# Two feed-forward layers behind a retention layer: when the weights' preparations are opened, and what stands ahead of what in the queues

## The chip, the cores and the metric

The kernel runs on one core of one Trainium2 chip. The metric is the device time of one execution in microseconds (us). One execution of the kernel was also profiled. TensorE (PE) does the matrix products, VectorE (DVE), ScalarE (ACT) and GpSimd (POOL) the elementwise work, and SyncE (SP) issues most DMA transfers. ACT issues some too, between its own instructions. Each engine works through its own instructions strictly in order, so an instruction that waits holds up everything behind it on that engine.

## The reference

A retention layer (attention with a decaying state, 4 sequences of 768 positions, 8 heads of 64) is followed by two feed-forward layers (3072 tokens, model width 512, hidden width 2048), all in float32:

```python
state = gamma[None, :, None, None] * state + np.einsum('bhd,bhe->bhde', k[:, :, t], v[:, :, t])
y[:, :, t] = scale * np.einsum('bhd,bhde->bhe', q[:, :, t], state)
...
x = attn_out.transpose(0, 2, 1, 3).reshape(B * S, H * D)
h = x @ w_in;  x = np.maximum(0.01 * h, h) @ w_out              # first layer
h = x @ w_in2; y = (h / (1.0 + np.exp(-1.702 * h))) @ w_out2    # second layer
```

## The kernel before

**Retention** runs in 24 steps of 128 positions. A step loads its q, k and v (1 MB, `a_load`) into one of the areas w4 to w7, which later hold weights. `a_scores` makes the masked scores of a step one step ahead, `a_decay` scales the keys on ACT, `a_out` makes the outputs and the new state, and `a_store` scales the outputs on DVE and, for all but the first sequence, writes them to DRAM with three transfers (`swapped`). `place(s)` says in which area a step's data stand: four areas in turn for the first eight steps, three (w5, w6, w7) after that. So a load is issued four steps ahead at first and three steps ahead later. The first seven steps run alone; the other 17 are fed in half steps between the products of the first layer.

**Each layer** has two stages. In `First`, the inputs times `w_in` go through the activation function and are stored to DRAM. In `Second`, those times `w_out`. Both use a scheme that multiplies 2 x 2 blocks with seven products of sums of blocks in place of eight; every float32 operand is split in a high and a low part, and a product takes three matmuls for each half of the inner dimension, six in all. `First` has 32 pairs (4 blocks of tokens, times 8 blocks q of the hidden width) of seven products each. I call one product, with the evacuations of PSUM behind it, a tick, because the function `tick` is called once behind each. In the first five pairs of the first layer (`one`) the products of a pair use each other's banks closely and the retention's half steps stand between them. From pair 5 on, the products of a pair and of the one before are interleaved, 1, 5, old 7, 2, 6, old 3, old 4. A copy on ACT (L479) of the first product's bank must be made before product 2 may add to that bank, and an add on DVE (L403) combines two banks. Before products of a new block begin, `early_sums` makes two sums of its inputs on POOL (L335, L336), at the pair q = 6.

**A weight's preparation** (`Prep`, one for each half of each block q, 16 for each of the four weight matrices) turns a stored 64-bit word into float32 and forms the seven sums of blocks. Its steps are: `load` (two transfers of 256 KB into a raw buffer), `open` (two ACT instructions, L169 and L170, that read the raw buffer and write into a result buffer), `word` (three DVE instructions, L173, L175, L177), `round_up` (one POOL instruction, L186, the last to read the raw buffer), `total` (three subtractions, L152 when on DVE or POOL) and then `store` (448 KB to DRAM), or `keep` (a cast on ACT, L155, and a subtraction on DVE, L152, straight into the weight's area), or `split` and `store_split` (a high and a low part in two result buffers, and two stores). Raw and result buffers are taken in turn from rings: in the first layer two, later three raw buffers and three result buffers (areas c1, ex and c2), in the second two raw and three result buffers.

The order of all this is written out by hand. `Later` is a table of steps that are due at a tick. The weights of the first layer's `First` (`own`, 16 preparations) have ticks of their own (`OWN_AT`: load, words with sums, keep). Of the other 48, 26 are made during the first layer's `First` and 22 during the second's. They come in bunches: `TODO1` and `TODO2` say at which pair one or two preparations are put into a queue (`behind`) as three pieces each, `open`, two of the `word` steps, and the third with rounding, sums and the `load` of a later preparation. One piece is taken from the queue at each tick, except in the pairs at a block's end and beginning. The store or keep follows five ticks behind the third piece.

```python
            def finish():
                self.word(2, 3)
                self.sums(e, e2)
                self.end(clock, keep)
                if others:
                    others.pop(0).load()

            return [self.open, lambda: self.word(2), finish]
```

`sums` is `round_up` on POOL and `total` right behind it: on DVE for the first layer's 26 and the second's first few, on POOL for `own` and for the rest.

Of the kernel before, what the change touches and what calls it, by code (L numbers as in the profile page):

```python
# [21 lines left out]
P = 128  # L22
# [16 lines left out]
def _word(bits):  # L39
# [20 lines left out]
EARLY_PREPS = ((3, 5), (4, 6))  # L60
EARLY_FORMS = ((1, 3), (2, 4), (5, 5), (6, 6))
OWN_AT = {2: (None, 0, 2), 3: (None, 2, 4), 4: (3, 6, 8), 5: (5, 8, 10), 6: (8, 11, 13), 7: (12, 15, 17), 8: (16, 19, 21),
          9: (20, 23, 25), 10: (23, 26, 31), 11: (26, 29, 32), 12: (28, 31, 34), 13: (30, 34, 38), 14: (32, 37, 42),
          15: (35, 41, 44)}
# [35 lines left out]
def retention_two_ffn(ctx: ExitStack, tc: tile.TileContext, qkv, consts, small, w1i, w1o, w2i, w2o, scratch, out):  # L100
# [87 lines left out]
    class Prep:  # L188
# [37 lines left out]
        def sums(self, e=nc.gpsimd, e2=None):  # L226
            round_up(self.f, self.low, e)
            self.total(e2 or e)

        def words(self):  # L230
            self.open()
            self.word(3)

# [16 lines left out]
        def end(self, clock, keep=False, ticks=5):  # L250
# [8 lines left out]
        def pieces(self, clock, others, e, e2, keep=False):  # L259
            def finish():  # L260
                self.word(2, 3)
                self.sums(e, e2)
                self.end(clock, keep)
                if others:
                    others.pop(0).load()

            return [self.open, lambda: self.word(2), finish]
# [432 lines left out]
    def early(s):  # L700

        for n, (words, keep) in enumerate(EARLY_PREPS):
            if s == words:
                own[n].words()
                own[n].sums()
            if s == keep:
                own[n].keep()
# [9 lines left out]
    def retention():  # L717
        place = lambda s: (5, 6, 7, 4)[s % 4] if s < 8 else 5 + (s - 8) % 3
# [71 lines left out]
        def a_store(s, o):  # L790
# [17 lines left out]
            swapped(xd0[b][:, :, c * P : c * P + P], x)  # L808
# [29 lines left out]
        for s in range(len(steps)):  # L838
# [9 lines left out]
            a_store(s, o)  # L848
# [144 lines left out]
    def step2(n):  # L993
# [4 lines left out]
        if n == 1:  # L998
            for p in todo[:2]:
                p.load()  # L1000
# [137 lines left out]
```

## Time and profile before

| | us |
|---|---|
| two timed executions | 1169.71, 1169.93 (median 1169.82) |
| the profiled execution, its own time | 1171.34 |
| span of its trace | 1169.6 |
| PE busy in it (91%) | 1063.1 |
| DVE busy (67%) | 778.4 |
| ACT busy (53%) | 617.3 |
| POOL busy (17%) | 193.6 |

The span is cut in stages, which follow each other: the first seven retention steps up to about 60 us; the first layer's `First` from 60 to 442, with the other retention steps in it up to about 177; its `Second` to 671; the second layer's `First` from 670.8 to 935.3; its `Second` to the end. A busy PE is no proof of a PE at full pace: matmuls overlap, and at half of the granted clock they take twice as long. So the number of matmuls in a stretch of time is read beside it.

### The profile page before, as it was taken

To read this page: it belongs to the slowest core of one execution; us is meant where nothing else is said; L and a number is where in the kernel's file an instruction comes from. 1 tells how busy PE (TensorE), PEld (TensorE's weight loads), DVE (VectorE), ACT (ScalarE), POOL (GpSimd) and SP (SyncE) were. 2 spreads that over 40 slices of the span, in tenths; PEclk is the share of its full clock that TensorE was granted. 3 is DMA by queue.
4 is the path that set the end of the run, shared out by engine and by line. 5 is a ranking of instruction groups with operands and counts; after the bars stand their busy time and mean duration, and the time that the engine had idled before them with its cause. 6 is when DMAs were issued, how large, how long until landed. Compare 5 with 4: busy or idle time off the path is not lost.

```text
span 1169.6 us, 17536 instructions
## 1 busy us (share of the span) xinstructions
PE 1063.1 (91%) x6150; PEld 943.3 (81%) x6151; DVE 778.4 (67%) x1255; ACT 617.3 (53%) x1223; POOL 193.6 (17%) x193
## 2 busy tenths in 40 slices
PE   8687886968877999999999997989899999999998
PEld 6566665968867998888888897989799988888886
DVE  5855454546546658978878857535343589788786
ACT  5644434635445676555454674645455655454543
POOL 0332126213223100000000003444450000000000
PEclk9988889987988999999999998999999999999999
DMA  8568754387677787372353784486747863753823
GB/s 322 193 208 301 244 178 152 126 279 246 211 252 251 247 304 230 99 248 79 127 187 89 249 284 145 152 287 207 267 177 228 260 198 117 178 154 72 218 73 72
DMA packets 190568, 231.37 MB, mean 198 GB/s; under 512 B 59152, under 2 KB 146192, under 8 KB 187408
## 3 DMA queue, kind: packets, MB, share of 16 engines
q1 hardware_dynamic: 148704, 179.08, 48.5%
q10 hardware_dynamic: 41776, 51.17, 12.2%
q8 instruction: 48, 0.79, 0.3%
q14 instruction: 40, 0.33, 0.1%
HBM read 141.46 MB, written 88.74 MB: 197 GB/s over the span
## 4 chain that ended last, share of the span: by engine, by line
PE 61%; DMA 17%; DVE 9%; ACT 4%; POOL 3%; issue 3%; SPq 1%; ACTq 1%; POOLq 0%; DVEq 0%
PE psum L599 37%; PE psum L374 22%; DMA w<-qkv 6%; DMA wd1o<-c 3%; POOL c L186 2%; DMA e<-w2o 2%; DMA a<-gd 1%; PE psum L747 1%; DVE w L152 1%; DMA c<-w1o 1%; DVE c L177 1%; DMA gd<-b 1%; DVE c L152 1%; DMA wd2i<-c 1%; DMA gd<-f 1%
## 5 line engine op out<-in xcount | busy, mean ns | idle before, releaser
L599 PE MATMUL psum<-c,w 128*128 128x512 f32 x1008 | 229.0, 389 | 0.0
L599 PEld LDWEIGHTS psum<-c,w 128*128 128x128 f32 x1008 | 189.1, 188 | 39.5 <-DVE c L152 0.2
L374 PE MATMUL psum<-a,w 128*128 128x384 f32 x576 | 120.7, 360 | 28.0 <-ACT psum L479 21.8
L374 PEld LDWEIGHTS psum<-a,w 128*128 128x128 f32 x576 | 107.5, 203 | 35.5 <-ACT psum L479 24.8
L599 PE MATMUL psum<-e,w 128*128 128x512 f32 x576 | 135.8, 389 | 0.0
L374 PE MATMUL psum<-c,w 128*128 128x384 f32 x576 | 115.8, 344 | 18.1 <-DVE d L403 17.8
L599 PEld LDWEIGHTS psum<-e,w 128*128 128x128 f32 x576 | 108.1, 188 | 22.4
L374 PEld LDWEIGHTS psum<-c,w 128*128 128x128 f32 x576 | 103.0, 193 | 21.4 <-DVE d L403 20.4
L374 PE MATMUL psum<-b,w 128*128 128x384 f32 x576 | 111.4, 337 | 0.8 <-ACT psum L479 0.8
L374 PEld LDWEIGHTS psum<-b,w 128*128 128x128 f32 x576 | 102.2, 190 | 1.1 <-ACT psum L479 1.1
L374 PE MATMUL psum<-e,w 128*128 128x384 f32 x384 | 81.5, 357 | 15.1 <-DVE b L403 4.8
L374 PE MATMUL psum<-d,w 128*128 128x384 f32 x384 | 83.2, 362 | 10.9 <-ACT w L155 8.5
L552 ACT CAST c<-b 128x512 fp32r<-128x512 f32 x96 | 59.4, 622 | 55.7 <-DVE c L152 30.3
L374 PEld LDWEIGHTS psum<-e,w 128*128 128x128 f32 x384 | 71.0, 201 | 20.0 <-DVE dx L403 6.4
L374 PEld LDWEIGHTS psum<-d,w 128*128 128x128 f32 x384 | 73.0, 205 | 14.8 <-ACT w L155 9.4
L186 POOL TENSOR_TENSOR c<-c,c 128x512 int32<-128x512 int32 x33 | 44.2, 1338 | 226.7 <-DVE c L177 140.4
L152 DVE TENSOR_TENSOR c<-b,c 128x512 fp32r<-128x512 f32 x96 | 65.5, 689 | 18.9 <-ACT c L552 16.9
L393 ACT ACTIVATE d<-psum 128x384 f32<-128x384 f32 x96 | 46.4, 490 | 50.1 <-PE psum L374 44.9
L152 DVE TENSOR_TENSOR w<-w 128x512 fp32r<-128x512 f32 (+3 forms) x102 | 48.1, 511 | 29.9 <-ACT w L288 23.9
L152 DVE TENSOR_TENSOR c<-c 128x128 f32<-128x128 f32 (+1 forms) x82 | 36.8, 449 | 44.8 <-POOL c L186 38.2
L758 ACT ACTIVATE w<-w,f 128x64 f32<-128x64 f32 x160 | 40.4, 335 | 44.2 <-DMA w<-qkv 37.2
L152 POOL TENSOR_TENSOR a<-a 128x768 f32<-128x768 f32 x7 | 13.2, 1890 | 277.3 <-DMA xd<-e 260.4
(200 smaller groups left out, 1779.4 us busy)
## 6 DMA issues: line engine op xcount, KB each, us to landing
gd<-d ACTq DMA_DIRECT2D x128, 192.0 KB, 3.2
w<-qkv SPq DMA_DIRECT2D x21, 1024.0 KB, 6.0
b<-gd SPq DMA_DIRECT2D x72, 256.0 KB, 4.1
d<-gd SPq DMA_DIRECT2D x54, 256.0 KB, 3.7
a<-gd SPq DMA_DIRECT2D x48, 256.0 KB, 4.8
gd<-dx ACTq DMA_DIRECT2D x47, 192.0 KB, 3.5
c<-w1i SPq DMA_DIRECT2D x32, 256.0 KB, 4.6
e<-w2o SPq DMA_DIRECT2D x32, 256.0 KB, 4.0
```

The source lines that it names most:

```text
L152: e.tensor_tensor(out=o, in0=x, in1=y, op=ALU.subtract)
L177: lambda f, high: nc.vector.scalar_tensor_tensor(out=f, in0=f, scalar=3, in1=high, op0=ALU.logical_shift_left, op1=ALU.bitwise_or))
L186: e.tensor_tensor(out=f.bitcast(I32), in0=f.bitcast(I32), in1=low.bitcast(I32), op=ALU.add)
L374: nc.tensor.matmul(out=t, lhsT=w[:, k, a], rhs=x[:, b, k], start=(start and m == 0), stop=(m == 5), skip_group_check=True)
L393: nc.scalar.activation(out=t, in_=x, func=self.func)
L552: nc.scalar.copy(out=t[:, 0], in_=self.block_of(*item))
L599: nc.tensor.matmul(out=t[:, j], lhsT=w[:, j, a], rhs=x[:, b], start=(new and q == 0 and m == 0), stop=(q == NQ - 1 and m == 2), skip_group ...
L747: nc.tensor.matmul(out=ps[:, e, n], lhsT=kT[r, n], rhs=qT[r, n], start=True, stop=True, skip_group_check=True)
L758: nc.scalar.activation(out=ks_t[s][:, h], in_=ks_t[s][:, h], func=AF.Copy, scale=kdec[:, c, h : h + 1])
```

## The change

- `own` preparations: the sums leave POOL for DVE, one or two ticks behind the words and rounding, and the keep follows at the tick of before, or for one of them a tick earlier. In the first steps `own_words` does the same through the table of due steps.
- The other 48 preparations no longer go through the queue. Each has a tick in `OPEN1` (five apart) or `OPEN2` (six, then eight apart), from which `plan` sets every step: the load 7 ticks (first layer) or 5 ticks (second) before, `open`, two word steps one tick later, the third word step and the rounding two ticks later, the sums on DVE four ticks later, the store five (or the keep six, or the split five and its stores seven).
- Retention: `a_load` is written ahead of the store of the same step, and the four areas are used for the first 16 steps.
- The second layer's result ring has two buffers in place of three, and its `First` eight buffers for the activated results (`g`) in place of five.

```diff
-OWN_AT = {2: (None, 0, 2), 3: (None, 2, 4), 4: (3, 6, 8), ...
-          9: (20, 23, 25), 10: (23, 26, 31), 11: (26, 29, 32), 12: (28, 31, 34), 13: (30, 34, 38), 14: (32, 37, 42),
-          15: (35, 41, 44)}
+OWN_AT = {2: (None, 0, 1, 2), 3: (None, 2, 1, 2), 4: (3, 6, 1, 2), ...
+          8: (16, 19, 1, 2), 9: (20, 23, 1, 2), 10: (23, 26, 1, 5), 11: (26, 29, 1, 3), 12: (28, 31, 1, 3),
+          13: (30, 34, 2, 4), 14: (32, 37, 2, 4), 15: (35, 41, 2, 3)}
-TODO1 = {**{n: 2 for n in (9, 10, 11, 12, 13, 14, 17, 18, 19, 20, 21)}, **{n: 1 for n in (22, 25, 26, 27)}}
-TODO2 = {2: 2, 4: 2, 5: 2, 6: 1, 9: 2, 10: 1, 11: 1, 12: 1, 13: 2, 14: 1, 17: 2, 18: 1, 19: 1, 20: 1, 21: 1, 22: 1}
+OPEN1 = (*range(54, 100, 5), *range(109, 157, 5), *range(165, 195, 5))
+OPEN2 = (10, 16, 22, 28, 34, 39, *range(53, 100, 8), *range(109, 158, 8), 165, 173, 181)
...
+        def own_words(self, clock, total, keep):
+            self.open()
+            self.word(3)
+            round_up(self.f, self.low, nc.gpsimd)
+            clock.at(total, lambda: self.total(nc.vector))
+            clock.at(keep, self.keep)
+
+        def last_word(self):
+            self.word(2, 3)
+            round_up(self.f, self.low, nc.gpsimd)
+
+        def plan(self, clock, at, lead, keep=False):
+            clock.at(at - lead, self.load)
+            clock.at(at, self.open)
+            clock.at(at + 1, lambda: self.word(2))
+            clock.at(at + 2, self.last_word)
+            clock.at(at + 4, lambda: self.total(nc.vector))
             if keep:
-                clock.at(ticks, self.keep)
+                clock.at(at + 6, self.keep)
             elif self.kind == "2i" and self.q < N_SPLIT:
-                clock.at(ticks - 1, self.split)
-                clock.at(ticks + 1, self.store_split)
+                clock.at(at + 5, self.split)
+                clock.at(at + 7, self.store_split)
             else:
-                clock.at(ticks, self.store)
+                clock.at(at + 5, self.store)
...
-        place = lambda s: (5, 6, 7, 4)[s % 4] if s < 8 else 5 + (s - 8) % 3
+        place = lambda s: (5, 6, 7, 4)[s % 4] if s < 16 else 5 + (s - 16) % 3
...
-            a_store(s, o)
+            put = a_store(s, o)
             if s + 2 < len(steps):
                 a_decay(s + 2)
-            n = s + 4 if s < 7 else s + 3
-            if s != 7 and n < len(steps):
+            n = s + 4 if s < 15 else s + 3
+            if s != 15 and n < len(steps):
                 a_load(n)
+            if put is not None:
+                put()
...
+    for p, at in zip(todo1, OPEN1):
+        p.plan(later, at, 7)
...
-                    "g": run_of(g_a2, 5, 1.5), "p": run_of(p_a2, 2, 1.5)},
+                    "g": run_of(g_a2, 8, 1.5), "p": run_of(p_a2, 2, 1.5)},
...
-    prep_rings2 = [ring(run_of(pe, 2, 4), 4, P, 2), ring([(pe, 8), (pex, 0), (g_a2, 8)], 8, P)]
+    prep_rings2 = [ring(run_of(pe, 2, 4), 4, P, 2), ring([(pe, 8), (pex, 0)], 8, P)]
...
+    for p, at in zip(todo, OPEN2):
+        p.plan(later2, at, 5, p.kind == "2i")
```

Three places show the order of instructions. Line numbers are a few lower in the changed kernel: L169, L170 (`open`), L173, L175, L177 (`word`), L152 (`total`) and L403 (`add`) of before are L168, L169, L172, L174, L176, L151 and L400 there. `c_315` is the result ring, `c_94` and `ex` are raw buffers, `psum` the banks.

DVE, in the middle of the first layer's `First`, before:

```order
L173 TENSOR_SCALAR c_315<-c_315 128x512
L175 TENSOR_SCALAR ex<-c_315 128x512
L177 SCALAR_TENSOR_TENSOR c_315<-c_315,ex 128x512
L152 TENSOR_TENSOR c_315<-c_315 128x256
L152 TENSOR_TENSOR c_315<-c_315 128x128 x2
```

The same place, changed:

```order
L172 TENSOR_SCALAR c_315<-c_315 128x512
L174 TENSOR_SCALAR ex<-c_315 128x512
L400 TENSOR_TENSOR f<-psum,f 128x384
L176 SCALAR_TENSOR_TENSOR c_315<-c_315,ex 128x512
L400 TENSOR_TENSOR psum<-psum,f 128x384
L151 TENSOR_TENSOR c_315<-c_315 128x256
L151 TENSOR_TENSOR c_315<-c_315 128x128 x2
```

The three subtractions stood right behind the last word step, whose result POOL still has to round. Now an add of the products stands between them.

ACT, in the first layer's last block, where the split preparations are (`L155` before and `L154` changed is the cast of `split`, `w_426` or `w_425` a weight's area), before:

```order
L155 CAST c_315<-c_315 128x896
L386 DMA gd_74<-f 128x384
L288 CAST w_426<-w_426 128x384 x2
L485 COPY f<-psum 128x384
L386 DMA gd_74<-f 128x384
L169 ACTIVATE c_315<-ex 128x512
```

Changed:

```order
L154 CAST c_315<-c_315 128x896
L168 ACTIVATE c_315<-c_94 128x512
L169 ACTIVATE c_94<-c_94 128x512
L476 COPY psum<-psum 128x384
L383 DMA gd_74<-f 128x384
```

The next `open` stands right behind the cast of the split; both write into a result buffer of the same ring.

SP, in the retention beside the first layer (`L737` or `L731` is `a_load`, `L162` and `L164` or `L161` and `L163` the store of a step, `L204` or `L203` a weight's load), before:

```order
L162 DMA xd_1_67<-w_84 256x1x128
L164 DMA xd_1_67<-w_84 128x1x128 x2
L737 DMA w_84<-qkv 128x2048
L162 DMA xd_1_67<-w_79 256x1x128
L164 DMA xd_1_67<-w_79 128x1x128 x2
L737 DMA w_77<-qkv 128x2048
```

Changed:

```order
L731 DMA w_84<-qkv 128x2048
L161 DMA xd_1_67<-w_84 256x1x128
L163 DMA xd_1_67<-w_84 128x1x128 x2
L203 DMA c_94<-w1i 128x2x256 x2
L731 DMA w_77<-qkv 128x2048
L161 DMA xd_0_66<-w_79 256x1x128
```

The load of a later step now stands ahead of the step's own store.

## Rows read from the trace of the kernel before

**Rows 1.** Matmuls of line 374 (products of `First`) alone, in stretches of us.

```profile
184.20:210.40 26.20, 18.70 (x85) 17.27 (x85) 0.87 0.37 119
225.00:292.70 67.70, 53.31 (x253) 50.46 (x252) 0.85 0.79 256
307.30:375.30 68.00, 51.09 (x253) 47.71 (x252) 0.87 0.76 259
397.20:416.20 19.00, 15.65 (x87) 14.46 (x86) 1.00 1.04 385
...
846.50:912.00 65.50, 65.50 (x380) 65.50 (x379) 1.00 0.64 216
670.80:935.30 264.50, 244.05 (x1344) 239.06 (x1343) 0.97 0.66 221
```

**Rows 2.** Waits of ACT, 225 to 375.3: us in total, times, longest.

```profile
ACT c L169 <- DMA wd1o<-c: 30.9, 10, 9.4
ACT c L169 <- DMA wd2i<-c: 11.5, 4, 4.0
ACT c L169 <- DMA c<-w1o: 8.0, 1, 8.0
```

**Rows 3.** Waits of DVE, the same stretch.

```profile
DVE c L152 <- POOL c L186: 33.8, 23, 1.5
```

**Rows 4.** Timeline 245 to 275: start, duration, instruction, [idle before <- releaser].

```profile
249.04 1.07 DVE L152 TENSOR_TENSOR c<-c 128x256 f32<-128x256 f32 x3 [1.46 <-POOL c L186]
...
261.97 0.66 ACT L169 ACTIVATE c<-ex 128x512 f32<-128x512 f32 x1 [4.38 <-DMA wd1o<-c]
...
263.83 0.49 ACT L479 COPY psum<-psum 128x384 f32<-128x384 f32 x1
...
264.38 4.21 PE L374 MATMUL psum<-a,w 128*128 128x384 f32 x12 [2.36 <-ACT psum L479]
```

**Rows 5.** DMA issues: size of each, median us from issue to landing.

```profile
gd<-dx ACTq DMA_DIRECT2D x47, 192.0 KB, 3.5
...
e<-w2o SPq DMA_DIRECT2D x32, 256.0 KB, 4.0
...
wd1o<-c SPq DMA_DIRECT2D x16, 448.0 KB, 5.8
...
c<-w1o SPq DMA_DIRECT2D x22, 256.0 KB, 4.3
```

**Rows 6.** Timeline 719 to 732, POOL and DVE.

```profile
722.82 1.83 POOL L335 TENSOR_TENSOR a<-a 128x768 f32<-128x768 f32 x1
722.90 4.21 DVE L152 TENSOR_TENSOR d<-d 128x256 f32<-128x256 f32 x3 [1.48 <-POOL d L186]
```

**Rows 7.** Waits of ACT, 670 to 935.

```profile
ACT e L169 <- DMA e<-w2o: 11.1, 3, 7.6
ACT ex L169 <- DMA gd<-d: 6.2, 1, 6.2
ACT d L169 <- DMA e<-w2o: 5.4, 2, 3.3
```

**Rows 8.** Timeline 176 to 200, the last keeps of `own`.

```profile
184.61 2.28 POOL L152 TENSOR_TENSOR c<-c 128x256 f32<-128x256 f32 x3
...
187.91 0.62 PE L374 MATMUL psum<-d,w 128*128 128x384 f32 x2 [3.04 <-ACT w L155]
```

**Rows 9.** Waits of PE, 62 to 200.

```profile
PE psum L747 <- DMA w<-qkv: 17.8, 8, 3.9
```

**Rows 10.** Timeline 100 to 132, one retention step's store and the load behind it.

```profile
104.20 0.68 DVE L805 TENSOR_TENSOR w<-psum,f 128x512 f32<-128x512 f32 x1
...
107.39 0.61 SPq L737 DMA_DIRECT2D w<-qkv  x1
```

**Rows 11.** Stretches: busy PE, PEld, DVE, ACT, POOL; granted clock, DMA share, GB/s.

```profile
60.00:176.80 116.80, 95.25 (x1049) 79.68 (x1050) 61.74 (x90) 49.75 (x133) 27.86 (x36) 0.87 0.73 236
...
400.00:420.00 20.00, 16.65 (x92) 15.49 (x92) 12.46 (x24) 13.66 (x28) 1.30 (x1) 1.00 1.03 368
...
30.00:60.00 30.00, 19.00 (x250) 15.36 (x250) 26.19 (x38) 18.79 (x49) 11.93 (x14) 0.93 0.55 178
```

More of the change, by code (lines that the diff above doesn't have):

```diff
@@ L224, in total @@
             subtract(f[:, 7], f[:, b21], f[:, 6], e)
[L226 to L232, printed above, removed]
         def store(self):
@@ L700, in early @@
     def early(s):
-        for n, (words, keep) in enumerate(EARLY_PREPS):
+        for n, words in enumerate(EARLY_PREPS):
             if s == words:
[L704 to L707, printed above, removed]
+                own[n].own_words(later, 1, 2)
         if s in EARLY_LOADS:
@@ L860, in retention_two_ffn @@
             early(k // 2)
-    behind1, todo1, waiting1 = collections.deque(), [], []
+    behind1 = collections.deque()
     for k, i in enumerate(FORMS[4:]):
         first1.form(0, i, (2 * k, 2 * k, 2 * k + 1), e=nc.vector)
-    for n, (load, words, keep) in OWN_AT.items():
+    for n, (load, words, total, keep) in OWN_AT.items():
         if load is not None:
             later.at(load, own[n].load)
-        if words is not None:
-            later.at(words, own[n].words)
-            later.at(words, own[n].sums)
-        if keep is not None:
-            later.at(keep, own[n].keep)
-    todo1.extend(names["1o"] + names["2i"][2 * N_SPLIT : N_IN1] + names["2i"][: 2 * N_SPLIT])
-    def start1(behind, todo, waiting, k, clock, e, e2, keep=lambda p: False):
-        for _ in range(k):
-            if todo:
-                p = todo.pop(0)
-                behind.extend(p.pieces(clock, waiting, e, e2, keep(p)))
+        later.at(words, lambda p=own[n], a=total, b=keep: p.own_words(later, a, b))
+    todo1 = names["1o"] + names["2i"][2 * N_SPLIT : N_IN1] + names["2i"][: 2 * N_SPLIT]
+    assert len(todo1) <= len(OPEN1)
+    for p, at in zip(todo1, OPEN1):
+        p.plan(later, at, 7)
     x_a, y_a, z_a, u_a = [[(Area(t), n) for t, n in k] for k in
@@ L896, in step1 @@
             first1.g = ring(run_of(g_a[0], 2, 1.5) + run_of(few, 2, 1.5, 3) + (run_of(g_a[1], 2, 1.5) if n == 28 else []), T1)
-        if n in (6, 7):
-            for p in todo1[0:2] if n == 6 else todo1[2:3]:
-                p.load()
-            waiting1[:] = todo1[3:]
-        if n in TODO1:
-            start1(behind1, todo1, waiting1, TODO1[n], later, nc.gpsimd, nc.vector)
         if n == 26:
@@ L922, in retention_two_ffn @@
         behind1.popleft()()
-    assert not todo1 and not waiting1
     SPLITS2 = {3: [(6, 6, 7)], 4: [(7, 6, 7)], 10: [(6, 3, 4)], 11: [(7, 3, 4)], 18: [(6, 0, 1)], 19: [(7, 0, 1)],
@@ L988, in retention_two_ffn @@
     later2.at(2, lambda: w_split(2, 2, 3))
[L989 removed]
+    behind = collections.deque()
     todo = [Prep("2i", n, prep_rings2) for n in range(N_IN1, 2 * NQ)] + [Prep("2o", n, prep_rings2) for n in range(2 * NQ)]
[L991 removed]
+    assert len(todo) == len(OPEN2)
+    for p, at in zip(todo, OPEN2):
+        p.plan(later2, at, 5, p.kind == "2i")
     def step2(n):
@@ L997, in step2 @@
             behind.extend(w_steps(n + 2, 3, 7) + w_steps(n + 2, 0, 3))
-        if n == 1:
-            for p in todo[:2]:
-                p.load()
-            waiting.extend(todo[2:])
-        if n in TODO2:
-            start1(behind, todo, waiting, TODO2[n], later2, nc.gpsimd, nc.vector if n < 6 else nc.gpsimd,
-                   lambda p: p.kind == "2i")
         if n == 26:
@@ L1010, in retention_two_ffn @@
         behind.popleft()()
-    assert not todo and not waiting
     ident = t_a.view(0, P)
```

17 lines of the change are left out of this document (3 added, 14 removed).

## The prediction

> **What bounds the kernel now.** PE sets the end: outside of a few places its next matmul waits for nothing but the one before. So I read first how fast the products of `First` go, stretch by stretch, by their count. In the second layer 380 matmuls take 65.5 us, nine pairs, with PE busy throughout and a granted clock of 1.00 [rows 1]: 65.5 / 9 = 7.28 us for a pair, 1.04 for a tick. Held against that, the same work is late elsewhere [rows 1]:
>
> - first layer, pairs 10 to 15 (67.7 us) and 18 to 23 (68.0), six pairs each: 67.7 + 68.0 - 12 x 7.28 = 48.3 us lost;
> - pairs 6 and 7: 26.2 - 14.6 = 11.6 lost;
> - two pairs in the last block: 19.0 - 14.6 = 4.4 lost;
> - the whole `First` of the second layer: 264.5 - 32 x 7.28 = 31.5 lost.
>
> The clock column belongs to this: 0.85 to 0.87 in the bad stretches. A stall is followed by matmuls at half clock, and both are in the sums above.
>
> Next, who is late. In the two bad stretches ACT waits at `open`, 50.4 us in all over three rows [rows 2], nearly what PE loses there. Most is for the store of a preparation (wd1o, wd2i) that still reads the result buffer. The releaser's row with c<-w1o is a load. DVE waits 23 times for the rounding on POOL, 33.8 us [rows 3], with the adds of the products queued behind. One instance shows the whole chain [rows 4]: `open` at 261.97 had waited 4.38 us for a store. The bank copy L479 stood behind it on ACT and came at 263.83. PE had idled 2.36 us for it, and then its twelve matmuls took 4.21 us, at half clock.
>
> Why is the store always late? With one piece a tick and three result buffers, a buffer is opened again nine ticks after its last opening. Its store is issued seven ticks after, so two ticks, 2.1 us, are left for a store whose median landing is 5.8 us [rows 5]. The wait is built into the schedule. Preparations in pairs without a bunch cost nothing.
>
> **The change, part by part.** All sums are against the profiled execution, 1171.3 us; it lies 1.5 above the median.
>
> *The first layer's bunches.* Five ticks apart, a buffer returns after 15 ticks and its store is issued after five: ten ticks, 10.4 us, for a landing of 5.8. The load has seven ticks, 7.3 us, for 4.3 [rows 5]. The sums follow the rounding by two ticks, which covers the 1.46 us of the wait [rows 4]. So all three waits go. What is late next? `early_sums` is issued on POOL at pairs 14 and 22, in front of a rounding due a tick later. Its two instructions take some 3.7 us (the first 1.83), and beside them three subtractions on DVE took 4.21 us where they otherwise take 1.07 [rows 6, 4]. I put 3 us of PE on each of the two places, half clock included, and 6 us for stores and loads that land later than the median. 48.3 becomes 12: **-36** (bounds -20, if the rings still wait at every third opening, and -46).
>
> On those subtractions the Trainium skill, page "SBUF — State Buffer", section "Who interferes with whom", has a rule that speaks against moving sums to DVE: a DVE instruction with two SBUF inputs contends with a GpSimd instruction that reads SBUF, and the second to start blocks fully. The 4.21 us agree with it. By it the move is free wherever POOL is idle two ticks after a rounding, and costs a POOL instruction at the places named; without it those places would cost only the queue on POOL, some 2 us less each.
>
> *The first layer's last block.* Its last four preparations are split, and a split takes a second buffer of the same ring of three. Five ticks apart, that leaves three ticks, 3.1 us, between the two stores and the reuse, for a landing like the 5.8 of the other stores [rows 5]: about 2.5 us of ACT at three ticks. Before, such preparations stood seven ticks apart, and the block lost 4.4. **+2** (-2 to +6).
>
> *The second layer.* Here `open` waits for loads and stores, over the three largest rows 22.7 us [rows 7], because a load is issued as soon as a raw buffer is free and the bunch is opened at once. Now a load has five ticks, 5.2 us, for 4.0 [rows 5], and preparations stand six to eight ticks apart. Two result buffers are enough: eight ticks apart one returns after 16, and its store is issued after five, so 11 ticks are left. The 16 sums that move from POOL to DVE cost 16 x 1.07 = 17 us of DVE, beside products during which DVE is mostly idle. Remnants: the keep of the last weight is due at tick 45, one tick before pair 7 uses it, so a cast and a subtraction are waited for (2.5 us); `early_sums` at two places (6); the ends (1). 31.5 becomes 9.5: **-22** (-14 to -28). The eight buffers for results are of use only where a buffer's store was waited for; I count nothing, since I expect those waits to go with the bunches.
>
> *Keeps of the first layer.* Pairs 6 and 7 each wait for a keep whose sums POOL made in 2.28 us; PE waited 3.04 at one of them [rows 8]. On DVE the sums take 1.07, and the next rounding is free earlier. But the ticks of words and keep stay, so the chain is still longer than the room before the pair. **-5** (-2 to -9).
>
> *Retention.* PE waits 17.8 us for q, k and v in 62 to 200 [rows 9]. For one step the store's data were ready at 104.88, and the load behind the three store transfers was issued at 107.39 [rows 10]: 2.5 us earlier if it goes first, and DVE's scaling need not be awaited either, some 3.5 in all. And steps 8 to 15 get a fourth area, so a whole step of about 7 us (116.8 / 17) [rows 11] of head start. The stores come later by one transfer's issue, and nobody waits for them soon. 14 sums more on DVE are 15 us on 61.7 busy of 116.8 [rows 11]. I take two thirds of the 17.8: **-12** (0, if the transfers are the limit, to -22, all of it with the clock of 0.87 mended).
>
> *The first 60 us.* DVE is the busiest engine there, 26.19 of 30 us [rows 11], and gets the sums of two preparations, 2 x 1.07: **+2** (0 to +4).
>
> Sum: -36 + 2 - 22 - 5 - 12 + 2 = **-71**, or 1100 for the profiled execution and **1099** for the median.
>
> **Rivals.** *The transfers become the limit.* The same bytes in less time: per five ticks 960 KB for a preparation and 549 KB of results (192 KB four times a pair [rows 5]), 1.55 MB in 5.2 us, near 300 GB/s, and some 27 more for the block's inputs. The highest shown are 368 to 385 GB/s, at a DMA share above 1 [rows 11, 1]. At seven eighths of that, landings stretch, and the worst of the waits for a store was 9.4 us [rows 2]. If the bunches then keep 25 us more, and retention gains half: 71 - 31 = -40, 1130. For it: the pace. Against: ten ticks for a store in place of two. The Trainium skill, "DMA: Bandwidth & Descriptors", sections "Specifications" and "Latency and other measured facts", gives about 358 GB/s as a core's HBM limit and says that access latency grows from 0.2 to 2 us under load. By an estimate from that page the pace is at nine tenths of the limit, and every store would land up to 1.8 us later, still within its ten ticks.
>
> *All stalls go*, remnants too, and retention gains the whole: -36 - 10 - 22 - 6 - 9 - 20 = -103, 1067.
>
> *The waits change places*: the fixed ticks hold, but DVE and ACT now wait for POOL's rounding or a late load where they waited for stores, and little comes of it: -15, 1155. Against it: POOL is busy 27.86 of 116.8 us [rows 11], and gets less to do.
>
> *Slower.* An opening at a fixed tick blocks ACT if its buffer is not free. The bunches lost 48.3 us over some 20 openings, 2.4 us each; 48 openings now have fixed ticks. If each cost as much, that is 115 us, where those stages lost 84 before; with the other gains lost to the same transfers the kernel comes out 31 later, at 1200. It decides once the mean landing of a store passes its 10.4 us, against a median of 5.8 [rows 5].
>
> **How the numbers follow.** The forecast has 0.54 (1082 to 1116), the transfers' limit 0.19 (1116 to 1146), all stalls gone 0.16 (1060 to 1082), the waits in other places 0.08, slower 0.03. From 1064 to 1136 lie the first, two thirds of the second (0.13) and four fifths of the third (0.13): 0.80. About 2% (1146 to 1193) is what a measurement of this kernel can tell from no change. Faster by more: 0.89; within: 0.08; slower: 0.03.
>
> **What would show it.** Right: in pairs 10 to 23 of the first layer no wait of ACT's `open` for wd1o over 1 us on average, DVE's waits for POOL's rounding near nothing outside of pairs 14 and 22, a granted clock near 1.00, and a span of 45 us instead of 67.7 for six pairs. The second layer's `First` near 243 us. PE's wait for q, k, v under 6 us. Wrong: landings of stores near 10 us with the DMA share near 1; waits for loads in place of those for stores; a stage from 60 to 177 as long as before, with no wait for q, k, v, which would mean that DVE or the order of the half steps sets its pace; the first 60 us longer by more than 4.

## The result, and the profile after

The changed kernel takes 1103.12 us (1103.02 and 1103.22; the profiled execution 1103.22) against 1169.82. The ratio is 0.943, with a 95% interval of 0.939 to 0.947. The forecast was 1099.

The head of the page after: span, then busy time of each engine, its share and its instructions.

```profile
span 1101.5 us, 17557 instructions
PE 1041.2 (95%) x6150; PEld 925.6 (84%) x6151; DVE 823.8 (75%) x1351; ACT 620.1 (56%) x1223; POOL 139.6 (13%) x97
```

PE does the same 6150 matmuls in 22 us less of busy time, at a mean granted clock of 0.978 in place of 0.957; the other 46 us are idle time that has gone.

The changed kernel, matmuls of the products of `First` (now L371) alone, in stretches of us: length, PE busy, granted clock, DMA share, GB/s. They answer to [rows 1].

```profile
60.00:163.70 103.70, 47.27 (x210) 0.95 0.84 267
163.70:189.30 25.60, 20.29 (x86) 0.80 0.37 121
189.30:312.50 123.20, 118.58 (x675) 1.00 0.83 281
268.00:312.50 44.50, 44.50 (x259) 1.00 0.91 321
312.50:390.40 77.90, 65.42 (x355) 0.96 0.84 287
619.60:866.80 247.20, 239.85 (x1344) 0.98 0.71 237
```

Row 3 holds pairs 8 to 23, that is, all bunches of before, in 123.2 us. The same 16 pairs took 164.9 before, and 16 x 7.28 = 116.5 would be no loss at all. In row 4 PE is busy from end to end at a clock of 1.00 while 321 GB/s are moved. Row 2, pairs 6 and 7, is hardly shorter than the 26.20 of before and at a lower clock, 0.80. Row 5, the last block with its last products, has grown: 66.4 before. Row 6 is the second layer's `First`, 264.5 before.

Waits in those pairs, 189 to 312.5 (total, times, longest). First ACT, then DVE, then SP's queue, as in [rows 2, 3]:

```profile
ACT c L168 <- DMA ex<-w1o: 4.0, 1, 4.0
...
ACT c L168 <- DMA c<-w1o: 2.2, 1, 2.2
```

```profile
DVE c L151 <- POOL c L185: 19.6, 16, 1.5
```

```profile
SPq L226 <- DVE c L151: 79.9, 16, 21.0
```

`open` waits for no store any more. DVE still waits for POOL's rounding, 1.2 us on average against 1.5 before, and at fewer preparations. SP waits longest of all, with a store at its head that DVE has yet to finish. PE's own waits in that stretch come to 4.5 us.

DMA issues after, as in [rows 5]: size, median us to landing. Results and loads land about 1 us later than before, stores of weights 2.1 us earlier.

```profile
gd<-dx ACTq DMA_DIRECT2D x47, 192.0 KB, 4.5
e<-w2o SPq DMA_DIRECT2D x32, 256.0 KB, 5.1
wd1o<-c SPq DMA_DIRECT2D x16, 448.0 KB, 3.7
...
c<-w1o SPq DMA_DIRECT2D x22, 256.0 KB, 5.3
```

PE's waits in 62 to 200 after, against [rows 9]. For q, k and v they fell from 17.8 to 4.7 us. Of the wait for an add on DVE, 4.6 us are one wait that the kernel before had as well (4.49 us, ended at 59.97, just ahead of this stretch); two shorter ones come to 3.3 us, where the kernel before had one of 0.7.

```profile
PE psum L371 <- DVE psum L400: 7.9, 3, 4.6
PE psum L741 <- DMA w<-qkv: 4.7, 4, 2.5
```

### The profile page after: what moved, and what is told of

It reads as the page before. It is cut to its first block, busy times and chain, and to the rows that moved or that the text cites. A ratio compares the mean times of both kernels' runs of the same rounds, so it can differ in the third digit from the quotient of the medians.

```text
span 1101.5 us, 17557 instructions
## 1 busy us (share of the span) xinstructions
PE 1041.2 (95%) x6150; PEld 925.6 (84%) x6151; DVE 823.8 (75%) x1351; ACT 620.1 (56%) x1223; POOL 139.6 (13%) x97
## 4 chain that ended last, share of the span: by engine, by line
PE 61%; DMA 14%; DVE 14%; ACT 4%; issue 2%; POOL 2%; SPq 1%; ACTq 1%; POOLq 0%; DVEq 0%
PE psum L596 39%; PE psum L371 20%; DMA w<-qkv 5%; DVE e L151 3%; DVE c L151 2%; DVE w L151 2%; POOL c L185 1%; DMA e<-w2o 1%; DMA e<-w2i 1%; DMA wd2o<-ex 1%; DVE ex L151 1%; PE psum L741 1%; DMA ex<-w2i 1%; DMA wds<-c 1%; DMA ex<-w1o 1%
## 5 line engine op out<-in xcount | busy, mean ns | idle before, releaser
L371 PE MATMUL psum<-a,w 128*128 128x384 f32 x576 | 115.4, 350 | 18.5 <-ACT psum L476 8.9
L596 PEld LDWEIGHTS psum<-e,w 128*128 128x128 f32 x576 | 108.0, 188 | 22.9 <-DVE e L151 0.5
L371 PEld LDWEIGHTS psum<-a,w 128*128 128x128 f32 x576 | 104.4, 196 | 23.2 <-ACT psum L476 10.6
L371 PE MATMUL psum<-c,w 128*128 128x384 f32 x576 | 112.9, 339 | 5.9 <-DVE d L400 4.5
L371 PE MATMUL psum<-b,w 128*128 128x384 f32 x576 | 111.1, 336 | 0.4 <-ACT psum L476 0.4
L371 PEld LDWEIGHTS psum<-c,w 128*128 128x128 f32 x576 | 101.6, 190 | 8.5 <-DVE d L400 6.3
L371 PEld LDWEIGHTS psum<-b,w 128*128 128x128 f32 x576 | 101.6, 189 | 0.8 <-ACT psum L476 0.7
L151 DVE TENSOR_TENSOR c<-c 128x256 f32<-128x256 f32 (+2 forms) x130 | 62.0, 477 | 37.6 <-POOL c L185 28.5
L371 PE MATMUL psum<-d,w 128*128 128x384 f32 x384 | 78.9, 349 | 8.2 <-DVE w L151 5.0
L371 PE MATMUL psum<-e,w 128*128 128x384 f32 x384 | 77.3, 345 | 6.5 <-DVE dx L400 2.4
L151 DVE TENSOR_TENSOR c<-b,c 128x512 fp32r<-128x512 f32 x96 | 65.6, 690 | 20.1 <-ACT c L549 18.1
L371 PEld LDWEIGHTS psum<-d,w 128*128 128x128 f32 x384 | 68.9, 194 | 12.3 <-DVE w L151 6.0
L371 PEld LDWEIGHTS psum<-e,w 128*128 128x128 f32 x384 | 68.4, 193 | 10.5 <-DVE dx L400 3.4
L151 DVE TENSOR_TENSOR w<-w 128x512 fp32r<-128x512 f32 (+3 forms) x102 | 50.3, 529 | 32.7 <-ACT w L285 26.2
L185 POOL TENSOR_TENSOR c<-c,c 128x512 int32<-128x512 int32 x33 | 48.0, 1456 | 210.0 <-DVE c L176 172.0
L549 ACT CAST e<-a 128x512 fp32r<-128x512 f32 x58 | 35.9, 622 | 33.2 <-PE psum L596 14.2
```

What stands on the lines that cost most here:

```text
L151: e.tensor_tensor(out=o, in0=x, in1=y, op=ALU.subtract)
L185: e.tensor_tensor(out=f.bitcast(I32), in0=f.bitcast(I32), in1=low.bitcast(I32), op=ALU.add)
L371: nc.tensor.matmul(out=t, lhsT=w[:, k, a], rhs=x[:, b, k], start=(start and m == 0), stop=(m == 5), skip_group_check=True)
L549: nc.scalar.copy(out=t[:, 0], in_=self.block_of(*item))
L596: nc.tensor.matmul(out=t[:, j], lhsT=w[:, j, a], rhs=x[:, b], start=(new and q == 0 and m == 0), stop=(q == NQ - 1 and m == 2), skip_group ...
```

## The experiments

Each kernel is the changed kernel with one edit, unless something else is said. All were timed against the kernel before on the same chip. The stages in us, from the starts of the products in each profiled execution: *ret* is the first product to pair 6, then pairs 6 and 7, 8 to 23, *last* is pair 24 to the end of the first layer's `First`, *2nd* the second layer's `First`.

| kernel | ret | 6, 7 | 8-23 | last | 2nd | median | ratio to before (95%) |
|---|---|---|---|---|---|---|---|
| before | 144.9 | 26.2 | 164.9 | 66.2 | 264.4 | 1169.8 | |
| changed | 123.4 | 25.6 | 123.2 | 77.8 | 247.1 | 1103.1 | 0.943 (0.939-0.947) |
| 1 sums at once | 123.9 | 25.4 | 133.7 | 77.5 | 250.5 | 1117.2 | 0.955 (0.952-0.958) |
| 2 late store | 122.5 | 25.6 | 126.9 | 78.6 | 244.8 | 1106.7 | 0.947 (0.944-0.950) |
| 3 load behind | 131.7 | 23.3 | 123.1 | 74.2 | 246.6 | 1106.0 | 0.946 (0.944-0.948) |
| 4 three areas | 134.9 | 23.4 | 122.7 | 76.7 | 247.4 | 1109.9 | 0.949 (0.947-0.952) |
| 8 new ticks | 124.1 | 23.8 | 128.7 | 76.1 | 247.5 | 1105.9 | 0.947 (0.942-0.952) |
| 9 five g | 122.3 | 24.0 | 123.0 | 77.2 | 248.8 | 1101.1 | 0.941 (0.938-0.943) |
| 10 own on POOL | 122.6 | 25.5 | 122.8 | 73.7 | 246.6 | 1097.7 | 0.939 (0.935-0.943) |
| 11 bunch pace | 123.1 | 25.5 | 143.6 | 69.5 | 247.3 | 1111.5 | 0.949 (0.945-0.954) |
| 12 and bunch store | 125.5 | 25.6 | 147.8 | 69.7 | 245.6 | 1117.7 | 0.957 (0.952-0.960) |
| 13 early on DVE | 123.1 | 24.6 | 128.4 | 71.1 | 243.2 | 1096.0 | 0.936 (0.934-0.938) |
| 14 and loads | 125.6 | 23.3 | 162.7 | 71.1 | 247.5 | 1137.6 | 0.970 (0.966-0.974) |
| 15 two together | 121.3 | 25.6 | 121.5 | 75.3 | 242.4 | 1090.9 | 0.931 (0.926-0.935) |

A stage that an edit doesn't touch shows what stages vary by between kernels: 0.5 us in pairs 8 to 23 (122.7 to 123.2), up to about 3 us in the others, and 4 us (73.7 to 77.8) in the last block.

### Sums two ticks earlier, store eight ticks later

1, the sums right behind the rounding:

```diff
-            clock.at(at + 4, lambda: self.total(nc.vector))
+            clock.at(at + 2, lambda: self.total(nc.vector))
```

> The changed kernel, with the sums of the 48 planned preparations two ticks earlier, right behind the rounding, so that DVE waits for POOL again as before. My theory: the bunches cost their time because a result buffer was opened again two ticks after its store was issued; DVE's wait of 1.47 us is hidden mostly. Then the time rises by 8 us at most, to 1103 to 1111. The rival: DVE's wait, with the adds of the products behind it, was the larger part. Then each of 48 sums costs up to 1.47 us of PE, half clock included, and the time is 1125 to 1140.

2, the first layer's stores written 13 ticks behind `open`, so that two ticks were to be left before the buffer is opened again, as before. One late store in the last block is issued after its buffer has been taken again, so one weight of the second layer is not the right one.

```diff
-                clock.at(at + 5, self.store)
+                clock.at(at + (13 if lead == 7 else 5), self.store)
```

> The changed kernel, with the first layer's stores of prepared weights eight ticks later (13 after the opening in place of 5), so that two ticks are left between a store and the next opening of its buffer, as in the bunches before. Nothing else is moved. My theory, the room for the store: ACT waits at opening for wd1o and wd2i again, some 2 to 4 us each, and most of the 41 us that the bunches gained is lost: 1128 to 1150. The rival, that the even spacing, the earlier loads or the sums behind the rounding made the gain: 1101 to 1108.

DVE's waits and the products' matmuls in the kernel with the sums at once:

```profile
DVE c L151 <- POOL c L185: 29.4, 20, 1.5
```

```profile
191.70:325.30 133.60, 122.71 (x673) 0.97 0.78 261
```

With the sums at once, pairs 8 to 23 lose 10.5 us again, a quarter of what the change gained in those pairs, and the second layer 3.4, little more than that stage varies by. The wait itself is as long at the longest; what differs is that the adds of the products stand behind it instead of ahead of it. The late store gives back 3.7 us of 41.7, with three waits of ACT for stores of wd1o, 7.4 us. But it did not make the test that it was meant for. A tick is a place in the order of an engine's instructions, and SP runs ahead of the products until it meets something to wait for: in this kernel, too, 15 of the 22 stores were issued within about 1 us of the end of their sums, the median at 0.2 us. Whether two ticks of room are too few for a store, this run can't say.

### The bunches' pace, then their loads

11, the openings of the first layer at the ticks at which the queue of before gave them out, two in a pair, and all else as planned:

```diff
-OPEN1 = (*range(54, 100, 5), *range(109, 157, 5), *range(165, 195, 5))
+OPEN1 = (*(7 * n + k for n in (9, 10, 11, 12, 13, 14, 17, 18, 19, 20, 21) for k in (-3, 0)),
+         *(7 * n - 3 for n in (22, 25, 26, 27)))
```

> The changed kernel with the first layer's openings at the ticks of the bunches again (two in a pair, three and four ticks apart, in pairs 9 to 14 and 17 to 21), all else planned as changed: load seven ticks ahead, sums four behind, store five behind. The late stores (two ticks of room, but five ticks apart) cost only 3.7 us in the middle stage, so room alone is not the cause. My theory now: pace. A result buffer is held some 12 us from opening to landing, three of them carry one opening each 4 us, and the bunches ask for one each 3.6. Then the middle stage rises from 123 to 140 to 155 us: 1118 to 1135. If the gain came from sums behind the rounding and loads issued ahead, it stays under 130: 1103 to 1110.

12, the same, with the sums at once and the store at seven ticks:

```diff
+            clock.at(at + (2 if lead == 7 else 4), lambda: self.total(nc.vector))
+                clock.at(at + (7 if lead == 7 else 5), self.store)
```

> As the run with the bunches' openings, and in the first layer the store at seven ticks and the sums right behind the rounding, as before; only the loads stay seven ticks ahead. If pace, room and sums together are the whole of the 41.8 us, the middle stage is back at 155 to 170 us, 1135 to 1150. If the early loads are a part of the gain, 140 to 155.

14, as 12, and a load is again written right behind the rounding that frees its buffer, three preparations earlier:

```diff
-        p.plan(later, at, 7)
+        p.plan(later, at, 7 if todo1.index(p) < 3 else 0)
+        if todo1.index(p) + 3 < len(todo1):
+            later.at(at + 2, todo1[todo1.index(p) + 3].load)
```

> The bunches' ticks with stores at seven ticks and sums at once (middle stage 147.8 us), and now also the load of the preparation three later issued at the rounding's own tick, as before the change, in place of seven ticks ahead of its use. This is the schedule of before, without its queue. If SP's wait for the rounding at each load is the rest (17 us), the middle stage comes to 158 to 168 us, 1128 to 1140. If not, it stays under 152 and the rest lies in the queue that gave out the pieces: which instruction of a tick stands first on ACT and DVE.

The last kernel, with loads at the rounding: products in pairs 8 to 23, then waits of ACT and of SP in 205 to 378.

```profile
191.10:353.80 162.70, 130.06 (x674) 0.93 0.71 236
```

```profile
ACT c L168 <- DMA wd1o<-c: 37.4, 10, 12.4
ACT c L168 <- DMA c<-w1o: 11.9, 1, 11.9
ACT c L168 <- DMA wd2i<-c: 7.0, 3, 3.4
```

```profile
SPq L206 <- POOL c L185: 68.9, 13, 14.1
SPq L203 <- POOL c L185: 38.8, 10, 9.1
```

The kernel before, SP's waits in 210.4 to 375.3:

```profile
SPq L207 <- POOL c L186: 69.4, 13, 13.9
SPq L204 <- POOL c L186: 39.5, 10, 9.5
```

Step by step the stage of before comes back: 123.2, then 143.6 by the pace (+20.4), 147.8 by sums and store (+4.2), 162.7 by the loads (+14.9), of 164.9 before. The waits of ACT are like those of [rows 2] again, and SP's are those of before almost to the number. This is what the prediction's working had passed over: SP works in order, and a load for a raw buffer that POOL had not yet read stood ahead of a store whose sums were done.

How late a store was can be read as the time from the end of its sums on DVE to its issue on SP. The store that the `open` of [rows 4] waited for had its sums at 250.11 (249.04 + 1.07). In the kernel before, SP first issued the two transfers of a load, right behind the next preparation's rounding:

```profile
254.31 0.89 SPq L207 DMA_DIRECT2D c<-w1o  x2
255.24 0.47 SPq L235 DMA_DIRECT2D wd1o<-c  x1
```

In 12 a store follows the end of its own sums at once:

```profile
236.04 1.08 DVE L151 TENSOR_TENSOR c<-c 128x256 f32<-128x256 f32 x3 [1.48 <-POOL c L185]
...
237.15 0.34 SPq L226 DMA_DIRECT2D wd1o<-c  x1
```

The median over the 22 stores (wd1o and wd2i) is 4.8 us before, 0.1 in the changed kernel, 0.2 in 11 and 12, and 5.1 in 14. Before, SP stood still at such loads for 108.9 us in those pairs. In 11 and 12 it still waited for POOL, 25.9 and 60.8 us in 205 to 360, but stores with their sums done hardly stood behind these loads. When ACT came to an `open` of before, the store had been issued 2.3 us earlier (median of the 14 waits for stores), and what was left of its landing was the wait.

Half of the pace's part, 10.4 us, lies in pairs 14 and 22, where `early_sums` runs: each takes 12.5 us in 11 and 7.3 in the changed kernel. In both kernels the three subtractions take 4.2 us there; in 11 PE then waits 2.98 us for an add behind them and goes on at half clock. The edits were undone in this one order, and loads right behind the rounding were not run at the even pace, so the parts may be others in another order.

### Retention: order and areas

3, the load behind the store of its step, as before; 4, the areas and the distance of before (four areas up to step 7, then three):

```diff
             put = a_store(s, o)
+            if put is not None:
+                put()
...
                 a_load(n)
-            if put is not None:
-                put()
```

```diff
-        place = lambda s: (5, 6, 7, 4)[s % 4] if s < 16 else 5 + (s - 16) % 3
+        place = lambda s: (5, 6, 7, 4)[s % 4] if s < 8 else 5 + (s - 8) % 3
...
-            n = s + 4 if s < 15 else s + 3
-            if s != 15 and n < len(steps):
+            n = s + 4 if s < 7 else s + 3
+            if s != 7 and n < len(steps):
```

> The changed kernel with the retention's loads behind the step's own store again, four areas kept. The stage from the first product to pair 6 fell from 144.9 to 123.3 us. If the order of the queue made the smaller part of that (a load some 3 us earlier, in a pipeline that has four areas of slack), this costs 0 to 6 us: 1103 to 1109. If the order made most of it: 12 to 18 us, 1115 to 1121.

> The changed kernel with the fourth area for the first 8 retention steps alone, as before, and the loads still in front of the stores. If the fourth area made most of the 21.6 us of the retention stage, this costs 10 to 16 us: 1113 to 1119. If the order of the queue made it, or the sums that left POOL: 0 to 5 us, 1103 to 1108.

PE's wait for q, k and v in 62 to 200, and the products from 60 to pair 6, first with the load behind the store, then with three areas:

```profile
PE psum L741 <- DMA w<-qkv: 9.2, 4, 3.3
```

```profile
60.00:172.20 112.20, 49.43 (x211) 0.91 0.77 256
```

```profile
PE psum L741 <- DMA w<-qkv: 11.5, 5, 3.2
```

```profile
60.00:176.40 116.40, 51.04 (x211) 0.88 0.77 249
```

Undoing the order costs 8.4 us of the stage, undoing the areas 11.6, together 20.0 of the 21.5 that the stage gained. The waits alone are 4.5 and 6.8 us longer; PE's busy time for the same matmuls is 4.2 and 7.6 us longer, at a granted clock of 0.91 and 0.88 in place of 0.95. Each of the two kernels gains 3 to 6 us elsewhere, in pairs 6 and 7 and in the last block, about what these vary by, so its whole time says less than its stage.

### Own sums on POOL, five g buffers

10 and 9:

```diff
-            clock.at(total, lambda: self.total(nc.vector))
+            clock.at(total, lambda: self.total(nc.gpsimd))
```

```diff
-                    "g": run_of(g_a2, 8, 1.5), "p": run_of(p_a2, 2, 1.5)},
+                    "g": run_of(g_a2, 5, 1.5), "p": run_of(p_a2, 2, 1.5)},
...
-    prep_rings2 = [ring(run_of(pe, 2, 4), 4, P, 2), ring([(pe, 8), (pex, 0)], 8, P)]
+    prep_rings2 = [ring(run_of(pe, 2, 4), 4, P, 2), ring([(pe, 8), (pex, 0), (g_a2, 8)], 8, P)]
```

> The changed kernel with the sums of the 16 own preparations on POOL again, at the same ticks. The order of the loads (8.4 us when undone) and the fourth area (11.6) already make 20 of the 21.5 us that the retention's stage gained, so I expect this to cost 0 to 5 us there and 2 to 4 at pairs 6 and 7: 1103 to 1111. The rival, that the two are one effect and POOL's sums were a large part: 10 us or more, 1113 or above.

> The changed kernel with five buffers for the second layer's activated results in place of eight, and the third result buffer of its preparations back. I expect no difference beyond 2 us in the second layer's first stage (247.1), and 1101 to 1106. The rival, that more buffers carried part of its 17.3 us: 251 or more.

Moving the own sums to DVE gained nothing: back on POOL, retention is 0.7 us shorter, pairs 6 and 7 are the same, and the median is 5.5 us lower, 4.1 of it in the last block, which has no own sums and varies that much. The g buffers are worth 1.7 us in the second layer's `First`, about what stages vary by.

### New ticks, and early_sums on DVE

8, openings from tick 50 without a gap between the blocks, splits eight apart, the second layer's keeps five apart and due before pair 6, the last own words up to five ticks earlier:

```diff
+          8: (16, 19, 1, 2), 9: (20, 23, 1, 2), 10: (23, 26, 1, 5), 11: (25, 28, 1, 4), 12: (27, 30, 1, 4),
+          13: (29, 32, 2, 4), 14: (31, 34, 2, 4), 15: (33, 36, 2, 4)}
+OPEN1 = (*range(50, 160, 5), 161, 169, 177, 185)
+OPEN2 = (8, 13, 18, 23, 28, 33, *range(53, 100, 8), *range(109, 158, 8), 165, 173, 181)
```

> The changed kernel with three places respaced, each in a stage of its own. (a) The first layer's last block: the 22 plain preparations five ticks apart from tick 50, the four split ones eight apart (161 to 185), so that a split's buffers have six ticks to land in place of three. If the split's ring is what lost 12 us there, the block falls from 77.8 to 66 to 70 us; if it is the traffic of the block as such, it stays within 3. (b) The second layer's first six openings five apart from tick 8, so that all sums are done before early_sums runs on POOL at tick 39 and the last keep is due at 39, seven ticks ahead of its use: 247.1 falls to 239 to 241, if sums beside POOL's reads (4.22 us for 1.07) made the stall at pair 6; if the keep as such is late, 245 or more. (c) The last own preparations two to five ticks earlier: pairs 6 and 7 fall from 25.6 to 16 to 20 us; if something else holds them, not under 24. All three: 1078 to 1090.

13, `early_sums` on DVE in the interleaved pairs, four splits seven apart, the other openings four or five apart; 15, `early_sums` on DVE and own sums on POOL at the ticks of the changed kernel:

```diff
-                        self.early_sums()
+                        self.early_sums(nc.vector)
```

```diff
+OPEN1 = (*(a + (9 * k + 1) // 2 for a in (54, 109) for k in range(11)), 165, 172, 179, 186)
```

> The changed kernel with two edits, read in different stages. (a) The sums of a new block's inputs (early_sums, at pairs 6, 14 and 22) on DVE in place of POOL, where they stood beside DVE's sums of a weight (4.2 us for 1.07, in the second layer at pair 6 with a keep behind them). If that meeting is what the second layer's pair 6 and 7 lose 8.8 us to, its stage falls from 247.1 to 239 to 242 us, and pairs 6 and 7 of the first layer gain 2 to 4; if DVE's own 1.9 us in the same place cost as much, within 2 us. (b) The first layer's preparations at ticks 54 to 99 and 109 to 154, eleven in each, 4 and 5 ticks apart, and the last four (split) at 165, 172, 179, 186. Then the last block has four preparations in place of six. If their number in that block is what costs, it falls from 77.8 to 68 to 71 us, as with the bunches' ticks (69.5); if it is the block's other traffic, not under 75. The middle stage may rise by up to 4. Both: 1087 to 1097.

> The changed kernel's ticks with two edits together: early_sums on DVE in the interleaved pairs, and the own preparations' sums back on POOL. If early_sums on POOL beside DVE's subtractions is what holds the second layer's First, that stage takes 243 us rather than 247 at the ticks of before, with no wait of PE's at pairs 6 and 7 over 2 us; if it was the new ticks of the run with both that helped, it stays at 247. The last block of the first layer: 71 to 74 us if early_sums is part of its loss, 77 if its loss is the splits alone. Own sums: retention's pairs within 1 us of the changed kernel's 123. Sum by the first: a median of about 1092; by the second, 1098.

The new ticks brought nothing in the second layer as a whole (247.5), although the last keep was due seven ticks before its pair. POOL began `early_sums` right behind the last rounding again and met the three subtractions, which took 4.21 us; pairs 6 and 7 take 20.3 us in place of 23.4, but pairs 0 to 5, with openings closer together, 45.7 in place of 41.8. In the first layer pairs 6 and 7 gained 1.8 us, within what they vary by, and where openings now fall on the blocks' ends the first pairs of the next blocks, 16 and 24, take 13.9 and 13.6 us in place of 7.6 and 7.3. `early_sums` on DVE did bring something, 3.9 us in the second layer with new ticks in the first layer and 4.7 with none, most of it in its pairs 6 and 7 (20.9 and 19.6 us). The kernel with both edits is the fastest of all: 1090.94 us, a ratio of 0.931 (0.926 to 0.935). Its stages:

```profile
159.80:185.40 25.60, 19.66 (x87) 0.80 0.37 122
185.40:306.80 121.40, 118.20 (x673) 1.00 0.84 286
306.80:382.10 75.30, 66.25 (x356) 0.95 0.85 289
611.40:853.80 242.40, 235.84 (x1343) 1.00 0.72 242
```

## Why the prediction was right, and where it was not

**The bunches, -36 forecast, -41.7 measured: the size was right and the reason only in part.** The runs give, in the one order in which the edits were undone, about half to the pace, a tenth to a quarter to sums behind the adds, and over a third to loads that no longer stand ahead of stores on SP. The step that failed is "the wait is built into the schedule", nine ticks less seven. ACT did come 2.3 us behind a store's issue, near the two ticks of the prediction, but the store was that late because SP held it behind loads, 4.8 us after its sums were done, and no term of the sum had that. Two more details were off. Sums two ticks behind the rounding were to cover the 1.46 us of the wait; on DVE only one add of a product stands between them, which takes half a microsecond, so DVE still waits 1.2 us, at 16 preparations. It costs little because the add is no longer behind, but "near nothing", as the sign was named, it is not. And the 6 us put on `early_sums` at pairs 14 and 22 were not lost: the sums do take 4.2 us there, but each of these pairs takes 7.3 us, as without any loss.

**The last block, +2 forecast, +11.6 measured, outside of its bounds.** The place was named and its price was not. The changed kernel, timeline 339 to 358 (start, duration, instruction, [idle before <- releaser]):

```profile
339.99 0.49 ACT L390 ACTIVATE f<-psum 128x384 f32<-128x384 f32 x1 [3.90 <-DMA gd<-f]
...
344.78 4.20 PE L371 MATMUL psum<-a,w 128*128 128x384 f32 x12 [4.77 <-ACT psum L476]
...
352.94 0.94 ACT L154 CAST c<-c 128x896 fp32r<-128x896 f32 x1 [4.63 <-DMA wds<-c]
...
357.23 0.96 PE L371 MATMUL psum<-a,w 128*128 128x384 f32 x4 [3.04 <-ACT psum L476]
```

ACT's waits in the whole block, 312.5 to 390.4:

```profile
ACT f L390 <- DMA gd<-f: 4.7, 2, 3.9
ACT c L154 <- DMA wds<-c: 4.6, 1, 4.6
...
ACT ex L390 <- DMA wds<-c: 2.5, 1, 2.5
```

I counted one wait of 2.5 us for the splits' ring. It is 4.6 us, and results on ACT wait three times, 7.2 us, for buffers that a store still reads. The transfers run at 359 GB/s and a DMA share of 1.01 in 340 to 360. The bank copy L476 stands behind such waits on ACT: PE idles 4.77 and 3.04 us, and twelve matmuls after it take 4.20 us, half clock. This fits the rival of the transfers, here in one block; but before the block had the same rates [rows 11] with less loss, so the rate is not the whole cause. With three preparations opened there (11) or four (13) in place of six, and the splits seven or more ticks apart, the block takes 69.5 and 71.1 us. In 8, with three opened and the split of a fourth, eight apart, it takes 76.1, of which the first pair alone takes 13.6. From pair 25 on it takes 62.4 us in 8, 62.2 in 11 and 63.9 in 13, against 70.5 in the changed kernel and 66.4 at the least in the kernels that keep its ticks. So fewer preparations with splits farther apart give back some 3 to 8 us; what part the distance has and what the number is open.

**The second layer, -22 forecast, -17.3 measured.** Of the 9.5 us that were to stay lost, 2.5 were put at the last keep, tick 45, and 6 at two `early_sums`. 14.1 stayed, 8.8 of them in pairs 6 and 7, where `early_sums` meets the sums that a keep waits for, and only 1.7 in pairs 8 to 23, which hold the other two `early_sums`. So the keep's term failed, which had the wait for one cast and not the sums ahead of it beside POOL. The changed kernel, timeline 661 to 674:

```profile
663.79 1.83 POOL L332 TENSOR_TENSOR a<-a 128x768 f32<-128x768 f32 x1
663.86 4.22 DVE L151 TENSOR_TENSOR e<-e 128x256 f32<-128x256 f32 x3 [1.47 <-POOL e L185]
...
665.70 1.90 POOL L333 TENSOR_TENSOR a<-a 128x768 f32<-128x768 f32 x1
...
668.16 0.94 ACT L154 CAST w<-e 128x896 fp32r<-128x896 f32 x1 [3.57 <-DVE e L151]
...
671.54 2.29 PE L371 MATMUL psum<-c,w 128*128 128x384 f32 x6 [3.76 <-DVE d L400]
```

The three subtractions take as long as both of POOL's instructions. The cast of the keep waits behind them on ACT, an activated result behind that, and PE stands 3.76 us and goes on at half clock. The Trainium skill, "SBUF — State Buffer", section "Who interferes with whom", says that a DVE instruction with two SBUF inputs contends with a GpSimd instruction that reads SBUF, and that the second to start blocks fully. The trace agrees: the first subtraction starts 0.07 us behind POOL's first instruction and ends 0.28 us behind its end, the second starts 0.24 us behind POOL's second and ends 0.14 us behind its end. Moving `early_sums` to DVE gave 3.9 and 4.7 us.

**Pairs 6 and 7, -5 forecast, -0.6 measured.** The changed kernel, timeline 160 to 172:

```profile
163.57 1.08 DVE L151 TENSOR_TENSOR c<-c 128x256 f32<-128x256 f32 x3 [1.21 <-POOL c L185]
...
165.73 0.62 PE L371 MATMUL psum<-d,w 128*128 128x384 f32 x2 [1.32 <-ACT w L154]
...
166.57 1.97 DVE L151 TENSOR_TENSOR w<-c,w 128x896 fp32r<-128x896 f32 x1
...
168.46 3.88 DVE L151 TENSOR_TENSOR c<-c 128x256 f32<-128x256 f32 x2
168.59 0.69 PE L371 MATMUL psum<-d,w 128*128 128x384 f32 x1 [2.24 <-DVE w L151]
```

The sums of the keep that PE waits for take 1.08 us on DVE instead of 2.28 on POOL, as forecast. But the words and keeps have the old ticks, and the keep's own subtraction took 1.97 us, beside a rounding on POOL, where at 161.28 it took 1.08. The one stall of 3.04 became two, 1.32 for the cast and 2.24 for the subtraction, and the stretch has a clock of 0.80. The sums of the next keep meet `early_sums` and take 3.88 us for the first two of three. The failed step is that a shorter link shortens the chain: with the sums on POOL again (10) the stage takes the same 25.5 us.

**Retention, -12 forecast, -21.5 measured, at its far bound.** The mechanism and both parts of it were right. Taking two thirds of the wait left out that its end mends the clock as well: 13.1 us of wait went, the clock rose from 0.88 to 0.95, and PE's busy time for the same matmuls fell by 6.6 us.

**The first 60 us, +2 forecast, +1.1 measured at the first product.** The terms sum to -68 against -71. The errors of +10 in the last block, +5 in the second layer and +4 in pairs 6 and 7 are nearly balanced by 9 in retention and 6 in the bunches, so it is luck in part that the total came within 4 us.

**The other rivals.** The transfers are not the limit in the bunches: at 321 GB/s PE waits for nothing. The Trainium skill, "DMA: Bandwidth & Descriptors", section "Specifications", gives a limit of about 358 GB/s for a core; the stretch with PE fully busy stays a tenth below it, and the 359 GB/s of the last block are at it. The 385 GB/s that the kernel before reached over 19 us [rows 1] lie above it, so for such stretches the measured figure counts. ACT's `open` waits for loads that have seven ticks, 7 us in all in pairs 8 to 23: fixed ticks did not bring the slower case.

## What to carry to other kernels

When an engine waits for a transfer, look first whether the transfer has been issued late: read the waits of the issuing queue, and keep whatever must wait for a buffer out of the way of what another engine needs soon. Spread periodic work at an even pace and write its dependent steps behind the work that would queue behind them; then a wait can stay as long as it is and cost nothing, as SP's 79.9 us here. A tick is a place in an engine's order and not a time: to know when a step ran, read the trace, as the store written eight ticks later and issued at once shows. Where half clock follows stalls, a term for a removed wait needs the clock's part as well, and a place that one names as a remnant needs the price of its whole chain up to PE, not that of the one wait.

## What was not expected of the hardware

Stores of the same 448 KB landed in 3.7 us (median) in the changed kernel and in 5.8 before, though more GB/s were moved (281 against 236 in pairs 8 to 23), while loads of 256 KB on the same queue went from 4.3 to 5.3. The bytes are the same, so how late a store lands hung on what was under way beside it more than on the mean rate. Part of it can be read: before, all 22 stores of wd1o and wd2i were issued while transfers of a weight's load were under way, and landed in 5.3 us (median); in the changed kernel 10 of the 22 found none under way and landed in 3.1, the other 12 in 4.6. That the loads are the cause is not shown. And DVE's three subtractions of the sums, 1.08 us alone, took 4.22 beside the two instructions of `early_sums` on POOL.
